# The last gates of the second group meet w_out as a split product in the third group's first period; weight splitting goes from two to three tiles a step

## The chip, the cores and the metric

One core of one Trainium2 chip runs the program. The metric is the device time of one execution in microseconds (us). Runs of one kernel differ by some us, so kernels are compared by the ratio of times taken in the same rounds.

In lines of the profile PE is TensorE (the matrix engine) and PEld its weight loads, DVE is VectorE, ACT is ScalarE, POOL is GpSimd, and SPq is the queue that issues the transfers. PSUM is the memory into which TensorE writes its sums. The granted clock is the share of its full clock that TensorE was given, 1.00 at most.

## The reference

```python
# q, k, v: (8, 8, 576, 64); w_in: (512, 2048), w_out: (2048, 512), both float64 in memory
kv  = einsum('bhsd,bhse->bhde', k, v)
out = einsum('bhsd,bhde->bhse', q, kv)
x   = out / sqrt(mean(out*out, -1) + 1e-6) * g_norm     # -> (4608, 512)
h   = x @ w_in
g   = h * erf(softplus(h))
y   = g @ w_out
```

## The kernel before

Tokens are taken in nine groups of 512. Hidden units come in 16 tiles of 128 (`FC`), four of them a batch (`BATCH`). Groups one and two use plain fp32 products. A full fp32 product of 128x128 by 128x512 is two records in the trace. From group three on each product is a Karatsuba split: every operand is held as a high part, a low part and their scaled sum, and three products of the rounded type fp32r replace one fp32 product. `n_ps` gathers two of them and `m_ps` the third.

A step is the work on one hidden tile; steps 0 to 15 are group one, 16 to 31 group two. In group two each step also splits two weight tiles. ACT rounds the high part (`w_upper`), VectorE makes the others one step later (`w_lower`), and a DMA writes the result to memory, from where the later groups load it. The stage through which this passes is a pool of buffers. Attention of the next group is woven into the steps, four steps for a pair of heads.

```python
    def w_upper(which, f):
        t = stage.tile([P, 3, G], FP32R, name="w_new", tag="w_new")
        ...
        upper(x, parts[:, 0])                       # ACT
        w_new[which, f] = t, x, [parts[:, i] for i in range(3)]

    def w_lower(which, f):
        t, x, parts = w_new.pop((which, f))
        lower(x, *parts)                            # VectorE, two instructions
        nc.vector.tensor_scalar(out=t[:, 1], in0=t[:, 1].bitcast(FP32),
                                scalar1=-SHIFT, scalar2=None, op0=ALU.mult)
        kept = w_kept[which, f] = dram.tile([P, 3, G], FP32, name=f"w_{which}{f}")
        nc.sync.dma_start(out=kept, in_=t.bitcast(FP32))
    ...
    for n in range(FIRST * FC + LAG):               # FIRST = 2 groups, LAG = 5 steps
        ...                                         # attention pieces of the next group
        if T < FIRST:
            ...                                     # h_ps: four fp32 products
            nc.scalar.copy(h, h_ps)
            nc.scalar.activation(s, h, AF.Softplus)
            for key in list(w_new):
                w_lower(*key)
            if T == FIRST - 1:
                for _ in range(2):
                    w_upper(*to_cut.pop(0))
            if f % BATCH == BATCH - 1:
                ...                                 # erf of the batch, tables
        if n >= LAG:
            T2, f2 = divmod(n - LAG, FC)
            project(f2, hs[n - LAG])                # o_ps: four fp32 products with w_out
            if f2 == FC - 1:
                store_first(T2)                     # out of PSUM and to memory, 1 MB
    ...
    for m in range(first_batch, batches + 1):       # a period: one batch of a later group
        for i in range(BATCH):
            n_ps, m_ps = hidden(T, b * BATCH + i)   # split products with w_in
            ...
        for j in range(J):                          # split products of the last period's gates
            if old_h is not None:
                result(T2, b2, j, g, w)
```

Each engine takes its instructions in the order written. The Trainium skill says it too ("TensorE: Matmul & The Clock Gate", section "Architectural detail: the array is 16× 32×32, not 1× 128×128": ACT and DVE queues are "strict FIFO").

## Time and profile before

| | before |
|---|---|
| time, median of 6 runs | 993.26 us (991.29 to 994.35) |
| TensorE busy, share of the profiled span of 990.5 us | 96% |
| VectorE, ACT busy | 75%, 62% |
| second group (130 to 262 us), TensorE busy | 131.91 of 132.00 us |
| second period of group three | 30.8 us, where a settled one takes 25.2 |

TensorE is the bound, the second group has no slack left on it, and the only thin place in the middle is the second period of group three. The first three of the six runs (median 994.19) are those the prediction knew.

### The profile page before, as it was taken

Reading aid. Unit: us, or ns where it says so; the run is one execution under the profiler, and the core shown is the slowest. Engines: PE = TensorE matmul, PEld = TensorE weight load, DVE = VectorE, ACT = ScalarE, POOL = GpSimd, SP = SyncE. Lnnn points to the kernel's source line nnn. Section 1 sums busy time; section 2 is a strip of 40 time slices with the busy share of each in tenths; the row PEclk is TensorE's granted clock in tenths of the full one; section 3 lists DMA queues with packets and bytes.
Section 4 is the critical chain, followed back from the end, with each engine's and each line's share of the span. In section 5 each row is a group of like instructions: output and inputs, shape, how many; then the busy total and the mean of one; then the engine's idle time right before and its main releaser. Section 6 shows DMA issues by size and latency. Waiting matters only on the chain.

```text
span 990.5 us, 11723 instructions
## 1 busy us (share of the span) xinstructions
PE 950.1 (96%) x4312; PEld 675.6 (68%) x4312; DVE 740.7 (75%) x1067; ACT 617.4 (62%) x821; POOL 2.4 (0%) x10
## 2 busy tenths in 40 slices
PE   6779999999998999999999999999999999989997
PEld 4334444444456778787778787878787787768885
DVE  2887896666845877777888777877778778886666
ACT  3688775677645666666666666666666666665551
POOL 0000000000000000000000000000000000000000
PEclk9899999999999999999999999999999999999999
DMA  9755514665679877898779877987796678657952
GB/s 273 233 165 165 164 41 176 251 235 226 272 268 381 312 280 266 262 368 294 274 244 355 310 283 241 347 304 284 248 330 254 252 257 337 264 222 295 358 200 74
DMA packets 100361, 256.63 MB, mean 259 GB/s; under 512 B 43984, under 2 KB 57296, under 8 KB 100304
## 3 DMA queue, kind: packets, MB, share of 16 engines
q1 hardware_dynamic: 98672, 253.59, 71.7%
q10 hardware_dynamic: 1568, 2.29, 0.8%
q8 instruction: 34, 0.56, 0.2%
q14 instruction: 23, 0.19, 0.1%
q0 software_dynamic: 64, 0.00, 0.0%
HBM read 221.25 MB, written 34.60 MB: 258 GB/s over the span
## 4 chain that ended last, share of the span: by engine, by line
PE 76%; DVE 14%; ACT 7%; DMA 2%; issue 1%; DVEq 0%
PE n_ps L411 32%; PE m_ps L411 16%; PE o_ps L451 10%; PE h_ps L573 9%; PE se_ps L302 3%; DVE e L394 3%; DVE h L693 2%; PE qt_ps L296 2%; PE kv_ps L274 2%; DVE h L394 1%; DVE u L342 1%; ACT s L675 1%; ACT s L680 1%; DVE x L351 1%; DVE u L339 1%
## 5 line engine op out<-in xcount | busy, mean ns | idle before, releaser
L411 PE MATMUL n_ps<-x_forms,w_in_parts 128*128 128x512 f32 x896 | 233.3, 402 | 3.0 <-ACT x_forms L376 2.8
L411 PE MATMUL n_ps<-w_out_parts,g_forms 128*128 128x512 f32 x896 | 223.3, 391 | 3.1 <-DMA w_out_parts<-w_out 3.1
L411 PEld LDWEIGHTS n_ps<-x_forms,w_in_parts 128*128 128x128 f32 x896 | 166.7, 188 | 47.5 <-issue 9.3
L411 PEld LDWEIGHTS n_ps<-w_out_parts,g_forms 128*128 128x128 f32 x896 | 169.0, 189 | 39.6 <-DMA w_out_parts<-w_out 3.9
L675 ACT ACTIVATE s<-h 128x512 f32<-128x512 f32 x112 | 70.8, 632 | 198.3 <-DVE h L394 198.3
L573 PE MATMUL h_ps<-xT,w_in_sb 128*128 128x512 f32 x256 | 119.8, 611 | 4.0 <-DVE qT L339 2.7
L411 PE MATMUL m_ps<-w_out_parts,g_forms 128*128 128x512 f32 x448 | 120.5, 391 | 0.0
L411 PE MATMUL m_ps<-x_forms,w_in_parts 128*128 128x512 f32 x448 | 120.0, 390 | 0.0
L394 DVE SCALAR_TENSOR_TENSOR h<-m_ps,h 128x512 f32<-128x512 f32 x112 | 77.1, 688 | 55.6 <-ACT h L673 45.5
L451 PE MATMUL o_ps<-w_out_sb,h_sb 128*128 128x512 f32 x256 | 114.8, 592 | 0.0
L379 DVE TENSOR_TENSOR g_forms<-h,g_forms 128x1024 fp32r<-128x1024 f32 x56 | 68.4, 1222 | 44.8 <-ACT g_forms L376 44.4
L411 PEld LDWEIGHTS m_ps<-w_out_parts,g_forms 128*128 128x128 f32 x448 | 84.4, 188 | 17.6
L411 PEld LDWEIGHTS m_ps<-x_forms,w_in_parts 128*128 128x128 f32 x448 | 84.1, 188 | 17.6
L573 PEld LDWEIGHTS h_ps<-xT,w_in_sb 128*128 128x128 f32 x256 | 49.2, 195 | 61.9 <-issue 54.1
L394 DVE SCALAR_TENSOR_TENSOR e<-m_ps,e 128x512 f32<-128x512 f32 x112 | 77.5, 692 | 16.9 <-PE m_ps L411 8.8
L451 PEld LDWEIGHTS o_ps<-w_out_sb,h_sb 128*128 128x128 f32 x256 | 48.6, 190 | 60.4 <-issue 56.4
L673 ACT ACTIVATE h<-n_ps 128x512 f32<-128x512 f32 x112 | 65.5, 585 | 18.9 <-PE n_ps L411 18.9
L394 DVE SCALAR_TENSOR_TENSOR e<-n_ps,e 128x512 f32<-128x512 f32 x84 | 57.5, 685 | 25.2 <-PE n_ps L411 25.2
L380 DVE SCALAR_TENSOR_TENSOR g_forms<-g_forms 128x1024 fp32r<-128x1024 f32 x56 | 68.6, 1225 | 1.9
L693 DVE TENSOR_TENSOR h<-h,s 128x1024 f32<-128x1024 f32 x56 | 65.9, 1218 | 3.1 <-ACT s L680 3.1
L376 ACT ACTIVATE g_forms<-h 128x1024 fp32r<-128x1024 f32 x56 | 58.9, 1052 | 7.8 <-DVE h L693 6.4
L103 ACT ACT_TABLE_LOAD x46 | 59.0, 1283 | 0.8
(80 smaller groups left out, 965.2 us busy)
## 6 DMA issues: line engine op xcount, KB each, us to landing
w_in_parts<-w_in SPq DMA_DIRECT2D x112, 768.0 KB, 6.3
w_out_parts<-w_out SPq DMA_DIRECT2D x112, 768.0 KB, 7.6
w_in<-w_new SPq DMA_DIRECT2D x16, 768.0 KB, 3.2
w_out<-w_new SPq DMA_DIRECT2D x16, 768.0 KB, 3.3
k_sb<-in_k_dram SPq DMA_DIRECT2D x29, 288.0 KB, 4.1
v_sb<-in_v_dram SPq DMA_DIRECT2D x29, 288.0 KB, 5.0
q_sb<-in_q_dram SPq DMA_DIRECT2D x32, 256.0 KB, 4.0
w_raw<-in_moe_w_out_dram SPq DMA_DIRECT2D x8, 1024.0 KB, 5.0
```

What stands on the lines that cost most here:

```text
L103: nc.scalar.preload_act_table_set("softplus")
L302: nc.tensor.matmul(o_ps, lhsT=bd, rhs=qT, start=True, stop=True)
L376: nc.scalar.activation(high, x, AF.Copy, scale=1.0 + 2.0**-13)
L379: nc.vector.tensor_tensor(out=low, in0=x, in1=high.bitcast(FP32), op=ALU.subtract)
L380: nc.vector.scalar_tensor_tensor(out=both, in0=low.bitcast(FP32), scalar=SHIFT, in1=high.bitcast(FP32), op0=ALU.mult, op1=ALU.add,)
L394: nc.vector.scalar_tensor_tensor(out=out_, in0=ps, scalar=scale, in1=out_, op0=ALU.mult, op1=ALU.add)
L411: nc.tensor.matmul(ps, lhsT=weights(form, k), rhs=moving(form, k), start=(form == forms[0] and k == 0), stop=(form == forms[-1] and k == 3),)
L451: nc.tensor.matmul(o_ps[j], lhsT=g[:, j * P : j * P + P], rhs=w_out_sb[:, f, :], start=(f == 0), stop=(f == FC - 1),)
L573: nc.tensor.matmul(h_ps, lhsT=w_in_sb[:, c, f * P : f * P + P], rhs=xT[T][:, c, :], start=(c == 0), stop=(c == KC - 1),)
L673: nc.scalar.activation(h[:, i], n_ps, AF.Copy, scale=1.0 - 1.0 / SHIFT)
L675: nc.scalar.activation(s[:, i], h[:, i], AF.Softplus)
L693: nc.vector.tensor_tensor(out=h[:, part], in0=h[:, part], in1=s[:, part], op=ALU.mult)
```

## The change

Four gate tiles (28 to 31) of group two stay back. They meet w_out as split products in the first period of group three, which had no such products of its own. The aim is cheaper products, and a first period that is like every other. For this the split weights must be in memory earlier, so three tiles are split a step, with five stage buffers instead of four. The split is scaled so that VectorE needs two instructions a tile instead of three, and the adds of `m_ps` out of PSUM need no factor. All tiles of w_in are now split before those of w_out. The rest of the change, cut here, moves buffers and the last attention pieces to make room.

```diff
-        upper(x, parts[:, 0])
+        upper_w(x, parts[:, 0])
...
-        lower(x, *parts)
-        nc.vector.tensor_scalar(
-            out=t[:, 1], in0=t[:, 1].bitcast(FP32), scalar1=-SHIFT, scalar2=None, op0=ALU.mult
-        )
+        lower_w(x, *parts)
...
-    to_cut = [(which, f) for f in range(FC) for which in ("in", "out")]
+    to_cut = [(which, f) for which in ("in", "out") for f in range(FC)]
+    whole = FIRST * FC - BATCH
-    for n in range(FIRST * FC + LAG):
+    for n in range(FIRST * FC + 1):
...
-            stage = stage_room.enter_context(tc.tile_pool(name="stage", bufs=4))
+            stage = stage_room.enter_context(tc.tile_pool(name="stage", bufs=5))
...
+            h = hs[n] = old_h[:, n - whole] if n >= whole else unit("h_sb")
...
             if T == FIRST - 1:
-                for _ in range(2):
-                    w_upper(*to_cut.pop(0))
+                for key in to_cut[:2]:
+                    w_upper(*key)
+                if not w_new and stage_room is not None:
+                    ...
+                    load_parts("in", BATCH)
...                                                 # erf of a batch, late attention pieces
+            if T == FIRST - 1:
+                for key in to_cut[2:3]:
+                    w_upper(*key)
+                del to_cut[:3]
...
+    load_parts("out", BATCH)
     for m in range(first_batch, batches + 1):
...
-            add_scaled(h[:, i], m_ps, 1.0 / SHIFT)
+            add(h[:, i], m_ps)
...
-            if old_h is not None:
-                result(T2, b2, j, g, w)
+            result(T2, b2, j, g, w)
```

More of the change, by code (lines that the diff above doesn't have):

```diff
@@ L86 @@
     dram = ctx.enter_context(tc.tile_pool(name="dram", bufs=1, space=bass.MemoryType.DRAM))
+    wide = ctx.enter_context(tc.tile_pool(name="wide", bufs=2, side="right"))
     room, early_room = (ctx.enter_context(ExitStack()) for _ in range(2))
     first_w = room.enter_context(tc.tile_pool(name="first_w", bufs=1, side="right"))
-    xp = room.enter_context(tc.tile_pool(name="xp", bufs=2, side="right"))
     gate = room.enter_context(tc.tile_pool(name="gate", bufs=7, side="right"))
@@ L346, in norm @@
                 if T not in xT:
-                    xT[T] = xp.tile([P, KC, G], FP32, name="xT", tag="xT")
+                    xT[T] = wide.tile([P, KC, G], FP32, name="xT", tag="h")
                 x = xT[T][:, p, :]
@@ L391, in thirds, with upper_w, lower_w @@
         lower(x, high, low, both)
+    def upper_w(x, high):
+        nc.scalar.activation(high, x, AF.Copy, scale=(1.0 + 2.0**-13) / SHIFT)
+    def lower_w(x, high, low, both):
+        nc.vector.scalar_tensor_tensor(
+            out=low, in0=high.bitcast(FP32), scalar=SHIFT, in1=x, op0=ALU.mult, op1=ALU.subtract
+        )
+        nc.vector.tensor_tensor(
+            out=both, in0=high.bitcast(FP32), in1=low.bitcast(FP32), op=ALU.subtract
+        )
     def add_scaled(out_, ps, scale):
@@ L396, in add_scaled, with add @@
         )
+    def add(out_, ps):
+        nc.vector.tensor_tensor(out=out_, in0=ps, in1=out_, op=ALU.add)
     banks = [(ps_h, "h"), (ps_h, "h")] + [(ps_o, f"o{i}") for i in range(4)]
@@ L445, with project @@
     o_ps = {}
-    def project(f, g):
+    def project(f, g, last):
         for j in range(J):
@@ L455, in project @@
                 start=(f == 0),
-                stop=(f == FC - 1),
+                stop=last,
             )
@@ L466, in store, with sums @@
             side.dma_start(out=out[first_row : first_row + R, :], in_=e[h * R : h * R + R, :])
-    def store_first(T):
+    es = {}
+    def sums():
         for j in range(J):
-            e = acc.tile([P, DM], FP32, name="e", tag="e")
+            e = es[j] = acc.tile([P, DM], FP32, name="e", tag="e")
             if j % 2:
@@ L474, in store_first @@
                 nc.vector.tensor_copy(out=e, in_=o_ps[j])
-            store(T, j, e)
     def unit(name):
@@ L504 @@
     }
+    w_seq["out"][:0] = [("out", f) for f in range(FC - BATCH, FC)]
     def load_parts(which, n):
@@ L517, in pieces_of @@
     def pieces_of(T):
-        steps = [[] for _ in range(FC + 1)]
+        steps = [([], []) for _ in range(FC + 1)]
         for p in range(NP):
-            products, apply, halve, mean, norm, split = attention(T, p)
-            for i, piece in enumerate((products, apply, halve, mean)):
-                steps[BATCH * p + (min(i + 1, 3) if T == 1 and p == 0 else i)].append(piece)
-            steps[BATCH * p + BATCH][:0] = [norm, split]
+            *four, norm, split = attention(T, p)
+            for i, piece in enumerate(four):
+                step = BATCH * p + i
+                if T == 1 and p == 0:
+                    step = min(i + 1, 3)
+                late_in = 0
+                if T == FIRST and p == NP - 1 and i == 3:
+                    step, late_in = step - 1, 1
+                steps[step][late_in].append(piece)
+            if T == FIRST and p == NP - 1:
+                steps[FC - 1][0].extend((norm, split))
+            else:
+                steps[BATCH * p + BATCH][0][:0] = [norm, split]
         return steps
-    to_cut = [(which, f) for f in range(FC) for which in ("in", "out")]
+    to_cut = [(which, f) for which in ("in", "out") for f in range(FC)]
     hs, ss = {}, {}
-    for n in range(FIRST * FC + LAG):
+    whole = FIRST * FC - BATCH
+    for n in range(FIRST * FC + 1):
         T, f = divmod(n, FC)
@@ L537 @@
             stage_room = ctx.enter_context(ExitStack())
-            stage = stage_room.enter_context(tc.tile_pool(name="stage", bufs=4))
-        if f == 0:
-            if T:
-                ends[0]()
-                if T < FIRST:
-                    ends[1]()
-            if T < FIRST:
-                if T + 1 == FIRST:
-                    x_forms[FIRST] = late.tile([P, 3, KC, G], FP32R, name="x_forms0")
-                *steps, ends = pieces_of(T + 1)
-        if T < FIRST:
-            for piece in steps[f]:
+            stage = stage_room.enter_context(tc.tile_pool(name="stage", bufs=5))
+            x_forms[FIRST] = late.tile([P, 3, KC, G], FP32R, name="x_forms0")
+        if T < FIRST:
+            if f == 0:
+                ends = steps[FC][0] if T else []
+                steps = pieces_of(T + 1)
+                steps[0][0][:0] = ends
+            for piece in steps[f][0]:
                 piece()
@@ L552 @@
             weights()
-        if n == FIRST * FC:
-            for key in list(w_new):
-                w_lower(*key)
-            stage_room.close()
-            w_in_p = ctx.enter_context(tc.tile_pool(name="w_in_p", bufs=BATCH))
-            load_parts("in", BATCH)
         done = n - LAG + 1
-        if 0 <= done < FIRST * FC:
+        if 0 <= done < whole:
             nc.vector.tensor_tensor(out=hs[done], in0=hs[done], in1=ss[done], op=ALU.mult)
-        if n == FIRST * FC + BATCH - 1:
-            ends[1]()
-        if n == FIRST * FC:
-            *steps, split = attention(FIRST + 1, 0)
-        elif T == FIRST:
-            for i in (f - 1,) if f < BATCH else (f - 1, f):
-                steps[i]()
         if T < FIRST:
@@ L579 @@
                 )
-            h, s = hs[n], ss[n] = unit("h_sb"), unit("s_sb")
+            if n == whole:
+                old_h = wide.tile([P, BATCH, G], FP32, name="h", tag="h")
+            h = hs[n] = old_h[:, n - whole] if n >= whole else unit("h_sb")
+            s = ss[n] = unit("s_sb")
             nc.scalar.copy(h, h_ps)
@@ L585 @@
             if T == FIRST - 1:
-                for _ in range(2):
-                    w_upper(*to_cut.pop(0))
+                for key in to_cut[:2]:
+                    w_upper(*key)
+                if not w_new and stage_room is not None:
+                    stage_room.close()
+                    stage_room = None
+                    w_in_p = ctx.enter_context(tc.tile_pool(name="w_in_p", bufs=BATCH))
+                    load_parts("in", BATCH)
             if f % BATCH == BATCH - 1:
@@ L591 @@
                 softplus_table()
+            for piece in steps[f][1]:
+                piece()
+            if T == FIRST - 1:
+                for key in to_cut[2:3]:
+                    w_upper(*key)
+                del to_cut[:3]
         if n >= LAG:
             T2, f2 = divmod(n - LAG, FC)
-            project(f2, hs[n - LAG])
-            if f2 == FC - 1:
-                store_first(T2)
+            last = n - LAG in (FC - 1, whole - 1)
+            project(f2, hs[n - LAG], last)
+            if last:
+                sums()
+                if T2 == 0:
+                    for j in range(J):
+                        store(T2, j, es.pop(j))
+    for n in range(whole, FIRST * FC):
+        nc.vector.tensor_tensor(out=hs[n], in0=hs[n], in1=ss[n], op=ALU.mult)
     room.close()
@@ L601 @@
     late_r = ctx.enter_context(tc.tile_pool(name="late_r", bufs=1, side="right"))
-    gate_r = ctx.enter_context(tc.tile_pool(name="gate_r", bufs=2, side="right"))
+    gate_r = ctx.enter_context(tc.tile_pool(name="gate_r", bufs=1, side="right"))
     w_out_p = ctx.enter_context(tc.tile_pool(name="w_out_p", bufs=7, side="right"))
@@ L614, in cut @@
         return t
-    es = {}
     def result(T, b, j, g, w):
@@ L626, in result @@
             nc.vector.tensor_scalar(
-                out=es[j], in0=ps[0], scalar1=1.0 - 1.0 / SHIFT, scalar2=None, op0=ALU.mult
+                out=es[j], in0=ps[0], scalar1=SHIFT - 1.0, scalar2=None, op0=ALU.mult
             )
         else:
-            add_scaled(es[j], ps[0], 1.0 - 1.0 / SHIFT)
-        add_scaled(es[j], ps[1], 1.0 / SHIFT)
+            add_scaled(es[j], ps[0], SHIFT - 1.0)
+        add(es[j], ps[1])
         if b == NB - 1:
             store(T, j, es.pop(j))
-    FETCH = (("in",) * 4 + ("", "out", "out", "out out"), (*("", "in", "in", "out"), *("in", "out", "in", "out out")))
-    old_h = None
+    FETCH = ("", "in", "in", "out", "in", "out", "in", "out out")
+    load_parts("out", BATCH)
     for m in range(first_batch, batches + 1):
@@ L641 @@
         if T + 1 < NG:
-            todo = list(attention(T + 1, b)) if m > first_batch else [split]
+            todo = list(attention(T + 1, b))
             if b == 0:
@@ L657, in fetch @@
         def fetch(place):
-            for which in FETCH[m > first_batch][place].split():
+            for which in FETCH[place].split():
                 load_parts(which, 1)
@@ L663 @@
         if m < batches:
-            h = gate_r.tile([P, BATCH, G], FP32, name="h", tag="h")
-            s = gate_r.tile([P, BATCH, G], FP32, name="s", tag="s", bufs=1)
+            h = wide.tile([P, BATCH, G], FP32, name="h", tag="h")
+            s = gate_r.tile([P, BATCH, G], FP32, name="s", tag="s")
         for i in range(BATCH):
@@ L669 @@
             fetch(i)
-            if old_h is not None and i < 2:
+            if i < 2:
                 g.append(cut(old_h, i))
             if m < batches:
-                nc.scalar.activation(h[:, i], n_ps, AF.Copy, scale=1.0 - 1.0 / SHIFT)
-                add_scaled(h[:, i], m_ps, 1.0 / SHIFT)
+                nc.scalar.activation(h[:, i], n_ps, AF.Copy, scale=SHIFT - 1.0)
+                add(h[:, i], m_ps)
                 nc.scalar.activation(s[:, i], h[:, i], AF.Softplus)
@@ L682 @@
                 softplus_table()
-        if old_h is not None:
-            T2, b2 = divmod(m - 1, NB)
-            w = [w_now["out", b2 * BATCH + f].pop(0).bitcast(FP32R) for f in range(BATCH)]
+        T2, b2 = divmod(m - 1, NB)
+        w = [w_now["out", b2 * BATCH + f].pop(0).bitcast(FP32R) for f in range(BATCH)]
         for j in range(J):
-            if old_h is not None:
-                result(T2, b2, j, g, w)
+            result(T2, b2, j, g, w)
             fetch(BATCH + j)
```

## The prediction

> **What bounds the kernel now.** I first read the busy shares of the page, then the busy times of each engine in stretches, then the chain of waits in order of time around the change, and last the instructions of TensorE there. The page gives the bound:
>
> ```profile
> PE 950.1 (96%) x4312; PEld 675.6 (68%) x4312; DVE 740.7 (75%) x1067; ACT 617.4 (62%) x821; POOL 2.4 (0%) x10
> ```
>
> TensorE (PE) is busy 96% of the 990.5 us, and its granted clock is 9 tenths or more nearly throughout, so only two things move the end: less matmul time, or fewer gaps on TensorE. The stretches (start:end, length, busy us of PE, PEld, DVE, ACT, POOL, granted clock, DMA share, GB/s) say where gaps are:
>
> ```profile
> 266.65:290.50 23.85, 23.85 (x85) 11.46 (x84) 11.60 (x22) 13.38 (x20) 0.00 (x0) 1.00 0.68 254
> 290.50:301.40 10.90, 10.90 (x50) 8.72 (x50) 4.08 (x7) 5.29 (x9) 0.00 (x0) 1.00 0.81 283
> 301.40:332.20 30.80, 27.26 (x161) 21.22 (x160) 22.36 (x30) 21.43 (x27) 0.00 (x0) 1.00 0.95 361
> 431.60:456.80 25.20, 25.19 (x133) 20.24 (x132) 20.07 (x30) 16.01 (x21) 0.00 (x0) 1.00 0.85 305
> ```
>
> The second group ends with a tail of plain fp32 products (266.65 to 290.50, TensorE full). Then the third group's first period does only its four hidden tiles (10.9 us), because no gates wait for it in split form. Its second period, the third row, takes 30.8 us where a settled one takes 25.2. In the chain of waits in order of time (start, us, what), the part that matters is:
>
> ```profile
> 263.38 3.43 PE h_ps L573 x8
> 266.81 6.87 PE o_ps L451 x16
> ...
> 275.22 3.44 PE o_ps L451 x8
> ...
> 279.74 6.87 PE o_ps L451 x16
> ...
> 287.07 3.43 PE o_ps L451 x8
> 290.50 1.85 PE n_ps L411 x8
> 292.35 0.91 PE m_ps L411 x4
> ...
> 302.90 1.28 ACT L680
> 304.19 2.02 ACT s L680 x2
> 306.22 1.28 ACT L103
> 307.52 0.64 ACT x_forms L376
> ```
>
> Here one fp32 step against w_out (four products, eight records) costs 3.43 us, and one split product with its n and m parts 1.85+0.91, or 1.81+0.91 = 2.72 us when settled. From 301 us on, the chain is no longer TensorE: the first period's erf and table load come straight before the second period's pieces, and TensorE waits for what is queued behind them. The timeline of TensorE gives the gaps in brackets:
>
> ```profile
> 310.02 0.43 PE L301 MATMUL kv_ps<-qT_last,bd_kv 128*128 128x64 f32 x2 [1.70 <-DVE bd_kv L289]
> 320.69 0.51 PE L323 MATMUL ms_ps<-sq_hi,mean_w 128*128 128x512 f32 x1 [1.11 <-DVE sq_hi L315]
> ```
>
> With 0.22, 0.18 and 0.34 us after these, 3.55 us is idle in that period.
>
> **What the Trainium skill says.** "VectorE: DVE Perf Modes", section "The perf-mode tier table (the rule you actually need)", gives tensor_scalar on fp32 in SBUF twice the base rate, tensor_tensor on fp32 only the base rate, and no gain on fp32 in PSUM. The trace agrees: the weight rescale (L437) takes 427 ns, tensor_tensor from SBUF (L379) 684, and tensor_scalar from PSUM (L626) 685. So turning the scaled add out of PSUM (688 ns) into a plain add saves nothing worth counting. "ScalarE: Activation LUTs", section "What ACT_TABLE_LOAD costs", gives 1283 ns and a drain of 1380 more for a switch. The trace has the 1283; the drain is not seen (a load from 269.16 ends at 270.44, erf starts at 270.45). "DMA: Bandwidth & Descriptors", section "Where 436 GB/s comes from", puts the fabric at 435 GB/s and HBM at some 358 per core. Here slices of 0.75 us between 200 and 230 us show up to 451 GB/s, so the measured figures decide, and I work with 400 as the ceiling that bursts can hold.
>
> **The change, part by part.**
>
> 1. Gates 28 to 31 of the second group no longer meet w_out in fp32 but split, in period one of the third group. Removed: 4 steps x 3.43 = 13.73 us of TensorE. Added: four results (one per 128 rows of output), each a split product: 4 x 2.72 = 10.88 us. TensorE saves 2.85 us, all of it on the path. Added elsewhere: two more cuts of the gates (ACT 2 x 1.05, DVE 2 x (1.22+1.22) = 4.9 us) and eight adds of about 0.69; they lie beside the hidden tiles as in every later period.
>
> 2. The first period becomes an ordinary one: hidden tiles, cuts, the next group's attention and four results. The order of instructions built from the changed kernel confirms that results now stand between hidden tiles of period one and those of period two, and that the last x parts are cut before the tail. This takes away the crowding that cost 3.55 us of gaps. From kv of period one to kv of period three I therefore count two settled periods, 2 x 25.2 = 50.4 us (two measured periods, 406.41 to 456.80, are 50.39 together). Before it stand steps 26 and 27 in fp32, 2 x 3.43 = 6.87; after it the kv and qt pieces up to the hidden tile, 1.6 (456.80 to 458.40). Sum 58.9 us. Before, the same work, from 266.65 to 332.20, took 65.55. Saving 6.7 us: 2.85 from the cheaper products, 3.55 from the gaps, some 0.3 from smaller ones.
>
> 3. Weight splits: three tiles a step for 11 steps instead of two for 16. VectorE loses the rescale, 32 x 0.427 = 13.7 us. Per step it has 3 x 1.38 = 4.15 us of splitting instead of 2 x 1.81 = 3.62, ACT 1.84 instead of 1.23. A step of TensorE is 30.45/4 = 7.6 us (160.98 to 191.43), and in 130 to 262 us TensorE is busy 131.91 of 132.00, so this stage has nothing to win. What it may lose: the tile of kv (bd_kv) was ready at 184.93, TensorE used it at 186.92; one more cut of 0.6 us ahead of it in ACT's queue leaves about 1.4 us. Writes: 3 x 0.786 MB in 7.6 us is 310 GB/s, with q, k, v some 340; below those 400. I count 0, with a tail to the bad side.
>
> 4. The copies of the four sums, the four late gate products, and new scales: copies 2 x 0.58 on ACT and 2 x 0.69 on DVE as before. Scaled parts change numbers and not counts, so 0.
>
> 5. Loads of the four w_out parts for period one. In the order of issues they wait for VectorE's last gate product, because their room is the old gates' room. Counting from the last fp32 hidden tile: fp32 steps end at 6.9; copies and four products of 0.69 on VectorE end at 9.6; first load out at 9.7. TensorE wants the parts at 6.9+1.5 (kv, qt)+4 x 2.72+1.1 (apply) = 20.4. That is 10.7 us for 3.1 MB; at 400 GB/s 7.9 us plus the 2 to 3 us that a load alone takes (3.2 for 0.786 MB). Just enough; I charge 0.3 us.
>
> Sum: 994.2 - 6.7 + 0.3 = 987.8, less a little for the spare VectorE time (0.2): **987.6 us**, 0.7% faster.
>
> **Rivals.** (a) A DMA wait takes the place of the crowding. For: DMA share 0.95 in the old second period, and median landing of a w_out load is 7.6 us on the page; period one carries 3.1 MB more than a settled one. Against: the first four w_in parts now load long before, while the engines of transfer idle (several empty slices in 285 to 320 us). It would leave 1 to 3 us at the first result, time 989 to 990.5. (b) Three splits a step throttle the second group: ACT waits for a stage buffer, the gate copies come late, TensorE stalls in each of three or four steps. For: at each fourth step ACT already has table, erf and softplus together. Against: 1.4 us of slack left and the writes below the ceiling. It would cost 1 to 4 us, time 988.5 to 991.5. (c) VectorE in period one is the bound: cut, hidden adds and late gate products queue up, and hi and lo of the mean come late. For: in the settled period hi and lo are ready (447.28) only 0.8 us before use (448.06). Against: the cut starts 3.7 us after kv by the count of part 5, the settled one 4.4 us after (436.06 from 431.62). It would return 1 to 1.5 us. (d) Gaps return fully and only 2.85 us stay: 991.3.
>
> **Range and chances.** Middle 987.6. The four rivals are one-sided, 1 to 4 us each and perhaps one in five each; better than counted is limited to about 2 us. The three runs before spread over 0.6 us. So 985.3 to 990.6 should hold 8 times in 10. Two per cent would be 19.9 us, more than everything that is touched; faster by over 2% 0.01, within 2% 0.98, slower 0.01.
>
> **What would show it.** Right: o_ps records 224 instead of 256, the n_ps and m_ps results 4 more tiles; no fp32 result after the second step behind the last h_ps; from that h_ps to the third period's first hidden tile 58 to 60 us; the 1.70 and 1.11 us gaps gone; still almost no idle TensorE from 130 to 262 us; the end of the kernel unchanged with its 3.1 us wait for w_out parts. Wrong: a bracket on the first n_ps of period one's results naming w_out_parts (a), brackets on kv_ps L303 or h_ps in the second group (b), one on ms_ps L325 in period one (c), or a settled period that is no longer 25.2 us, since I assume that nothing there changes.

## The result, and the profile after

| | before | after |
|---|---|---|
| time, median of 6 runs | 993.26 us | 991.13 us (989.59 to 993.23) |
| ratio | | 0.9981 (95%: 0.9965 to 0.9998) |

A ratio here is the mean time of one kernel's runs over the mean of the other's runs of the same rounds, so it is not quite the ratio of the medians. The gain is 0.2%, some 2 us; 0.7% had been predicted, and 991.13 lies above the range.

First, where in the program do the two traces part? The moment at which TensorE starts the mean of each pair of heads (ms_ps) is a good milestone, because it comes once a batch in both:

| milestone | before, us | after, us | after minus before |
|---|---|---|---|
| in the second group, pair two of the third group's attention | 201.33 | 201.49 | +0.16 |
| in the second group, pair three of the third group's attention | 231.89 | 236.93 | +5.04 |
| in group three, its third period | 347.05 | 345.30 | -1.75 |
| last pair of the eighth group | 775.62 | 773.45 | -2.17 |
| third pair of the ninth group | 847.27 | 845.13 | -2.14 |
| fourth pair of the ninth group | 871.55 | 870.43 | -1.12 |

Between the first and the second line something takes 4.9 us. Then the change gives back 6.8 us (from +5.04 to -1.75). Then little happens for 500 us. The busy times of the second group after the change (start:end, length, busy us of PE, PEld, DVE, ACT, POOL, granted clock, DMA share, GB/s), and those of the new first and second period:

```profile
130.00:262.00 132.00, 129.30 (x407) 59.78 (x406) 88.60 (x140) 85.95 (x127) 0.00 (x0) 0.99 0.64 250
278.55:303.62 25.07, 25.07 (x133) 20.17 (x132) 18.99 (x29) 16.07 (x22) 0.00 (x0) 1.00 0.87 325
303.62:328.82 25.20, 24.93 (x131) 20.09 (x130) 19.94 (x29) 16.02 (x21) 0.00 (x0) 1.00 1.02 365
```

The periods are settled ones, as intended: 25.07 and 25.20 us. The second group, full before, has lost 2.70 us of TensorE. TensorE's timeline after the change shows where (start, us, engine, line, what, count, in brackets the idle time before and who ended it):

```profile
220.71 0.43 PE L303 MATMUL kv_ps<-qT_last,bd_kv 128*128 128x64 f32 x2 [1.92 <-DVE qT_last L294]
220.99 1.46 PE L304 MATMUL se_ps<-qT,bd_kv 128*128 128x512 f32 x2
222.24 4.95 PE L582 MATMUL h_ps<-xT,w_in_sb 128*128 128x512 f32 x8
```

There is one gap of 1.92 us (0.37 and 0.34 us came shortly before it), and the eight h_ps records behind it take 4.95 us, where the same eight take 3.60 elsewhere. In the kernel before there is no gap at this place:

```profile
217.48 0.33 PE L301 MATMUL kv_ps<-qT_last,bd_kv 128*128 128x64 f32 x2
217.65 1.08 PE L302 MATMUL se_ps<-qT,bd_kv 128*128 128x512 f32 x2
218.56 3.60 PE L573 MATMUL h_ps<-xT,w_in_sb 128*128 128x512 f32 x8
```

Following the chain of waits in order of time back from that gap gives the cause:

```profile
198.76 0.70 DVE w_new L402
...
199.51 5.42 DMA w_in<-w_new
...
205.02 0.63 ACT w_new L396
205.65 0.02 issue
205.67 1.28 ACT L102
...
217.38 0.63 ACT w_new L396
218.01 0.53 ACT x_forms L378
...
219.99 0.13 DVE bd_kv L291
...
220.71 0.43 PE kv_ps L303 x2
```

A write of a split tile to memory, 5.42 us long here, holds ACT before the next tile. ACT then does the mean, the gates and the erf late, in their order. At 217.92 it rounds the x parts; before the change it did so at 212.93:

```profile
212.93 0.63 ACT L376 ACTIVATE x_forms<-x 128x512 fp32r<-128x512 f32 x1
```

VectorE copies bd_kv and qT_last behind that, and TensorE needs both. The waits of ACT between 180 and 225 us after the change (engine, line, for whom, us in total, times, longest):

```profile
ACT w_new L396 <- DMA w_in<-w_new: 6.3, 3, 3.8
ACT w_new L396 <- DVE e L490: 4.6, 1, 4.6
```

The four waits end at 191.16, 199.32, 203.12 and 205.02 us, in steps 20, 21 and 22. The wait of 4.6 us the profile puts down to a copy of VectorE that came last. By the times it is a write as well: VectorE finished the first tile of the step before at 187.7, its write was issued at 187.82, a write took 3.2 us before the change, and ACT went on at 191.16. And the memory traffic in two stretches, first of the kernel before, then after the change:

```profile
203.00:208.00 5.00, 5.00 (x13) 2.28 (x12) 3.33 (x6) 4.77 (x8) 0.00 (x0) 1.00 0.82 328
208.00:213.00 5.00, 5.00 (x38) 2.72 (x37) 0.00 (x0) 4.94 (x8) 0.00 (x0) 1.00 0.07 14
```

```profile
203.00:208.00 5.00, 5.00 (x13) 2.16 (x12) 3.68 (x6) 3.55 (x5) 0.00 (x0) 1.00 1.02 426
208.00:213.00 5.00, 4.29 (x36) 2.30 (x35) 2.14 (x3) 4.89 (x8) 0.00 (x0) 1.00 1.01 420
```

After the change the DMA engines run full, at 420 GB/s, up to 213 us. Before, they were done by 208. The median write of a split tile took 3.2 (w_in) and 3.3 us (w_out) from issue to landing before, 4.3 (w_in) and 5.2 (w_out) after.

**Theory A:** with three tiles a step the third tile needs the buffer of the previous step's first tile. That tile's write is not done in steps 20 to 22, the more so as the first group's results (1 MB) leave at the same time. ACT stands before it, and everything that ACT does later comes late. **Rival B:** the missing gain is lost to a clock that slows by chance, mostly in the last group. The profiled run shows such places (granted clock 0.91 from 880 to 900 us). **Rival C:** three splits are too much work for ACT and VectorE, whatever the buffers do.

### The profile page after: what moved, and what is told of

Read it like the earlier page. It is cut to its first block, busy times and chain, and to the rows that moved or that the text cites. A ratio compares the mean times of both kernels' runs of the same rounds, so it can differ in the third digit from the quotient of the medians.

```text
span 991.4 us, 11745 instructions
## 1 busy us (share of the span) xinstructions
PE 951.9 (96%) x4328; PEld 681.5 (69%) x4328; DVE 736.6 (74%) x1047; ACT 618.7 (62%) x822; POOL 2.4 (0%) x10
## 3 DMA queue, kind: packets, MB, share of 16 engines
q10 hardware_dynamic: 1568, 2.29, 0.8%
## 4 chain that ended last, share of the span: by engine, by line
PE 72%; DVE 15%; ACT 7%; DMA 3%; issue 2%; SPq 0%; DVEq 0%; ACTq 0%
PE n_ps L427 34%; PE m_ps L427 17%; PE h_ps L582 7%; PE o_ps L464 6%; DVE h L718 3%; PE se_ps L304 3%; DVE e L412 2%; PE qt_ps L298 2%; PE kv_ps L276 1%; DMA w_out_parts<-w_out 1%; DVE u L344 1%; DVE x L353 1%; DVE u L341 1%; DVE e L407 1%; ACT L105 1%
## 5 line engine op out<-in xcount | busy, mean ns | idle before, releaser
L427 PE MATMUL n_ps<-w_out_parts,g_forms 128*128 128x512 f32 x928 | 232.7, 393 | 3.0 <-DMA w_out_parts<-w_out 3.0
L427 PEld LDWEIGHTS n_ps<-w_out_parts,g_forms 128*128 128x128 f32 x928 | 175.6, 189 | 41.1 <-DMA w_out_parts<-w_out 3.8
L427 PE MATMUL m_ps<-w_out_parts,g_forms 128*128 128x512 f32 x464 | 125.0, 391 | 0.0
L412 DVE TENSOR_TENSOR h<-m_ps,h 128x512 f32<-128x512 f32 x112 | 77.1, 688 | 50.4 <-ACT h L700 47.1
L381 DVE TENSOR_TENSOR g_forms<-h,g_forms 128x1024 fp32r<-128x1024 f32 x58 | 70.9, 1223 | 46.9 <-ACT g_forms L378 46.6
L464 PE MATMUL o_ps<-w_out_sb,h_sb 128*128 128x512 f32 x224 | 100.5, 592 | 0.0
L427 PEld LDWEIGHTS m_ps<-w_out_parts,g_forms 128*128 128x128 f32 x464 | 87.8, 189 | 18.4
L412 DVE TENSOR_TENSOR e<-m_ps,e 128x512 f32<-128x512 f32 x116 | 80.3, 692 | 17.5 <-PE m_ps L427 9.3
L407 DVE SCALAR_TENSOR_TENSOR e<-n_ps,e 128x512 f32<-128x512 f32 x88 | 60.3, 686 | 28.8 <-PE n_ps L427 28.8
L464 PEld LDWEIGHTS o_ps<-w_out_sb,h_sb 128*128 128x128 f32 x224 | 42.5, 190 | 53.2 <-issue 49.5
L105 ACT ACT_TABLE_LOAD x45 | 57.7, 1283 | 0.8
```

What stands on the lines that cost most here:

```text
L105: nc.scalar.preload_act_table_set("softplus")
L381: nc.vector.tensor_tensor(out=low, in0=x, in1=high.bitcast(FP32), op=ALU.subtract)
L407: nc.vector.scalar_tensor_tensor(out=out_, in0=ps, scalar=scale, in1=out_, op0=ALU.mult, op1=ALU.add)
L412: nc.vector.tensor_tensor(out=out_, in0=ps, in1=out_, op=ALU.add)
L427: nc.tensor.matmul(ps, lhsT=weights(form, k), rhs=moving(form, k), start=(form == forms[0] and k == 0), stop=(form == forms[-1] and k == 3),)
L464: nc.tensor.matmul(o_ps[j], lhsT=g[:, j * P : j * P + P], rhs=w_out_sb[:, f, :], start=(f == 0), stop=last,)
```

## The experiments

All were run on one chip, each in five rounds with the kernel before. All gave correct results.

**1. The changed kernel once more.**

> The changed kernel once more, on the chip of the runs beside it. Theory A: ACT stands before a full stage (the third split tile of a step needs a buffer whose write to memory is not done), the tile bd_kv of the third pair of the third group's attention comes late, and TensorE loses about 5 us in the second group (2.6 us of gaps, the rest a slower clock after them). It expects the gap of about 1.9 us on kv_ps L303 again and a ratio to before of 0.998. Rival B: the missing gain is lost late, to clock dips in the last group that fall by chance. It expects other runs to show other times, with ratios from 0.993 to 0.999, and no steady gap in the second group.

Measured: 990.33 us median, ratio 0.9981 (0.9963 to 0.9999). The gap is there again. In this profile, however, no slow products follow:

```profile
222.81 0.43 PE L303 MATMUL kv_ps<-qT_last,bd_kv 128*128 128x64 f32 x2 [1.93 <-DVE qT_last L294]
223.09 1.08 PE L304 MATMUL se_ps<-qT,bd_kv 128*128 128x512 f32 x2
224.00 3.60 PE L582 MATMUL h_ps<-xT,w_in_sb 128*128 128x512 f32 x8
```

From pair two to pair three it is 33.76 us here, 35.44 in the first profile, and 30.56 before the change. So the stall costs 3.2 us in both profiles, and 1.7 us more in the one in which the clock falls behind it. In the first profile the granted clock was 0.50 from 222 to 224 us, and the slow stretch lasted about 3.4 us in all (221.5 to 225 us). The Trainium skill names such a gate ("TensorE: Matmul & The Clock Gate", section "What's actually happening") with a free-running window of some 3.4 us. In the ten kept traces, after the first 100 us, every slow stretch with products in it follows a gap of TensorE, and longer gaps have one more often: all 9 gaps of 2.6 us or more, 3 of the 16 from 1.6 to 2.0 us, 2 of the 35 from 1.0 to 1.3 us. This fits a window that does not start with the gap; that it is this window no run here shows. Rival B has a part in the spread between runs, not in the steady loss.

**2. Two tiles in steps 20 to 23.** The write traffic is thinned where the results leave; the splits end one step later.

```diff
+                each = 2 if FC + BATCH <= n < FC + 2 * BATCH else 3
                 for key in to_cut[:2]:
                     w_upper(*key)
...
-                for key in to_cut[2:3]:
+                for key in to_cut[2:each]:
                     w_upper(*key)
-                del to_cut[:3]
+                del to_cut[:each]
```

> The changed kernel, but only two tiles are split in steps 20 to 23, where the first group's results leave; the splits end one step later. Theory A expects no gap over 0.5 us on TensorE from 140 to 262 us, the third period's first hidden tile about 6.7 us earlier than before (325.5 instead of 332.2), and about 4.9 us less than the changed kernel: ratio to before about 0.993. Rival B expects the same time as the changed kernel within 1 us. Rival C (three splits a step are too much for ACT and VectorE themselves) expects most of the stall to move to step 28 and a gain under 2 us.

Measured: 985.83 us median, ratio 0.9934 (0.9921 to 0.9947). No wait of TensorE is left from 130 to 262 us, ACT waits 0.2 us for w_new in all, and pair two to pair three takes 30.56 us, exactly as before the change. The third period's first hidden tile starts at 324.83 us, where 325.5 was expected. The stretch over most of the second group:

```profile
130.00:255.00 125.00, 124.90 (x402) 58.38 (x401) 87.80 (x140) 85.63 (x127) 0.00 (x0) 1.00 0.61 239
```

This is what theory A asked for within 0.1%, and it speaks against rival B. The stall does not move to step 28 either, as rival C would have had it, though three tiles a step are split in eight of the twelve steps. The DMA engines still move 416 to 423 GB/s from 188 to 203 us here, so full transfers alone do no harm.

**3. Three tiles a step, the first group's results stored at step 28.**

```diff
-                if T2 == 0:
-                    for j in range(J):
-                        store(T2, j, es.pop(j))
+        if n == whole:
+            for j in range(J):
+                store(0, j, es.pop(j))
```

> The changed kernel with three splits a step, but the first group's four stores (1 MB) wait until step 28. If the write bandwidth is what fills the stage (theory A, bandwidth), the waits of ACT for w_new on a write fall from 13 us to under 5 and the gap on kv_ps L303 goes: 4 to 5 us less than the changed kernel, ratio about 0.993. If the number of stage buffers against the time of one write is what holds (theory A, buffers), the waits stay above 8 us and the gap shrinks but stays: 1 to 3 us less. Rival C (engine time) expects no change.

Measured: 987.13 us median, ratio 0.9950 (0.9936 to 0.9963). The gap on kv_ps fell from 1.92 to 0.71 us. The waits of ACT for w_new from 180 to 225 us:

```profile
ACT w_new L396 <- DMA w_out<-w_new: 4.8, 1, 4.8
ACT w_new L396 <- DVE e L490: 4.6, 1, 4.6
ACT w_new L396 <- DMA w_in<-w_new: 3.0, 2, 1.7
```

Of these the 4.8 us fall behind the critical chain (at 223 us). The changed kernel has the same wait in the same step, 24, up to 225.95 us, and no gap of TensorE follows it. So one such wait alone does no harm; in steps 20 to 22 the waits add up to 10.9 us, just before ACT has the mean, the tables and the erf to do. From pair two to pair three it takes 31.54 us here, 1.0 more than before the change; in the changed kernel it was 3.2 more. The 1 MB of results is worth about 3 us of the 5, the rest is the buffer that is asked for too soon: the wait of 4.6 us, in step 20, is unchanged, since it comes before the results leave. The answer is between the two forms of theory A. The waits on a write, 13.0 us from 130 to 275 us after the change, fall only to 11.0, as the form with the buffers had it; the gain is just over its 1 to 3 us. A sixth buffer would have been the direct test, but there is no room for it (36 KB a partition wanted, 32.2 left), so how much one more buffer alone would give stays open.

**4. The split alone, in the kernel before.** Scaled parts, three tiles a step, five buffers; the fp32 tail and the first period are as before.

> The kernel before with the new split alone (scaled parts, three tiles a step, five stage buffers, w_in first), its fp32 tail and its first period unchanged. Theory A expects the same stall in the second group and nothing gained elsewhere: 4 to 5 us more than before, ratio 1.004 to 1.005. Rivals B expects 1.000.

Measured: 997.42 us median, ratio 1.0050 (1.003 to 1.007). The gap is there with 1.93 us and the same 4.6, 3.8 and 4.7 us as ACT's longest waits; pair two to pair three takes 35.43 us, so the clock fell here too. The split alone explains the loss.

**5. The scaled parts alone, in the kernel before** (two tiles a step).

> The kernel before with the scaled parts alone: two VectorE instructions a weight tile instead of three (13.7 us of VectorE less), plain adds out of PSUM, two tiles a step as before. VectorE is not on the path in the second group, so both theories expect the time of before within 0.1%: ratio 0.999 to 1.001, no gap on TensorE from 140 to 262 us.

Measured: 993.20 us median, ratio 1.0006 (0.9991 to 1.0022). It is the same time, and no wait of TensorE in the second group. The scaled form is neither a gain nor the cause.

**6. The third tile rounded by GpSimd.** Writes and buffers are unchanged; only the engine that has to wait is another.

```diff
-        upper_w(x, parts[:, 0])
+        if third:
+            nc.gpsimd.tensor_scalar(
+                out=parts[:, 0], in0=x, scalar1=(1.0 + 2.0**-13) / SHIFT, scalar2=None, op0=ALU.mult
+            )
+        else:
+            upper_w(x, parts[:, 0])
```

> The changed kernel with three splits a step; the rounding of the third tile alone moves from ACT to GpSimd, which is idle. Writes and buffers stay as they are. If ACT standing in order before a full stage is what makes bd_kv late (theory A), ACT no longer waits on the third tile, the gap on kv_ps L303 (1.9 us) goes or falls under 0.5 us, and the time is 3 to 5 us under the changed kernel: ratio 0.993 to 0.995, if GpSimd rounds a 128x512 tile in under some 4 us. If VectorE's own load or the writes make bd_kv late whatever ACT does (rival C), the gap stays above 1.5 us and the ratio is 0.998.

Measured: 986.25 us median, ratio 0.9938 (0.9925 to 0.9952). No wait of TensorE is left in the second group. GpSimd took 1.49 us for a w_in tile at the median, and stood before DMA writes for 21.5 us in all. ACT still waited 6.2 us for its own two tiles, in six pieces of 1.4 us at most, without harm. So it is the order on ACT that carried the wait to TensorE: with the same three splits on VectorE and the same bytes the loss is gone. This rules out rival C for VectorE and for the writes by themselves. ACT has 0.6 us a step less to do here, and in steps 20 to 23 of experiment 2 as well, so these two runs alone do not exclude ACT's own work. Other figures speak against it. Four times 0.6 us is 2.4, while the x parts came 5.0 us late and ACT had stood still for 10.9 us before. In experiment 3 ACT has all its work and the gap shrinks to 0.71 us. In steps 24 to 27 of experiment 2 ACT rounds three tiles a step and no gap follows.

**7. The kernel before with its fp32 tail, and the split of experiment 2.**

> The kernel before, with its fp32 tail and its first period, and the split as in the version with two tiles in steps 20 to 23. If the whole gain of that version (ratio 0.993) comes from the gates that meet w_out in the third group's first period, and the split only has to be kept from stalling, this kernel has the time of before: ratio 0.999 to 1.001, no gap on TensorE in the second group, the gaps of 1.7 and 1.1 us in the second period still there. If an early end of the split is worth something by itself, it is faster than before by 1 us or more.

Measured: 992.63 us median, ratio 1.0009 (0.9994 to 1.0025). The second group has no wait of TensorE, and the two main gaps in the second period stay:

```profile
PE kv_ps L301 <- DVE bd_kv L289: 1.7, 1, 1.7
PE ms_ps L323 <- DVE sq_hi L315: 1.1, 1, 1.1
```

So the whole gain of experiment 2 comes from the gates that meet w_out later, and none from the split.

**8. Experiment 2, with the last four w_out loads in the buffers of w_in.** This goes beyond the change and asks what a gap costs.

```diff
-        pool = w_in_p if which == "in" else w_out_p
...
+                spare = which == "out" and len(w_seq["out"]) < BATCH
+                pool = w_in_p if which == "in" or spare else w_out_p
```

> The version with two tiles in steps 20 to 23, and the last four w_out loads put into the buffers of w_in, which nobody needs any more at that point, so that the last period does not wait for a w_out buffer. In the version without it that wait is 2.75 us near the end and the following products run at a slower clock (n_ps 2.29 for five and m_ps 1.83 for four, instead of 1.3 and 1.07). If the clock falls because of the gap, taking the gap away returns 4 to 4.5 us: ratio about 0.989. If the slow clock comes there whatever the gap, it returns 2.7: ratio about 0.9905.

Measured: 982.19 us median (981.54 to 987.57), ratio 0.9906 (0.9888 to 0.9924); it beats both kernels. The wait for w_out parts went, and another that it had hidden took part of its place:

```profile
PE n_ps L427 <- DVE g_forms L381: 1.0, 1, 1.0
```

So 1.75 of the 2.75 us of gap went. Between the medians it returned 3.6 us. The slow n_ps and m_ps behind the gap (2.29 and 1.83 us) became 1.19 for four and 1.21, and the granted clock is 1.00 there, so in this profile the slow clock went with the gap. The ratio is the smaller of the two expected; but a gap of 1 us is left, and one of the six runs (987.57) had a clock of 0.988, the others 0.994. Of the 4.45 us that the gap and the slow clock cost together, 3.4 should come back with 1 us of gap left, which the 3.6 between the medians agrees with; 1.75 would come back if the slow clock came whatever the gap. The expectation "4 to 4.5 us" was a little too high.

## Why the prediction was wrong

**What bounds the kernel, and the saving of part 2: right.** From the last h_ps of the second group to the third period's first hidden tile it took 58.75 us (271.68 to 330.43); 58.9 was predicted, 65.55 it was before. Experiment 2, in which nothing disturbs this, gains 0.66%, or 6.6 us of 992.24; the predicted saving was 6.7. The o_ps records are 224, and the n_ps records with w_out 928 instead of 896, as the list of signs had them. Experiment 7 shows that this gain belongs to the moved gates.

**Part 1, 2.85 us by cheaper products: agrees with the trace.** The first results take 1.83+0.91 us each, as counted. How the 6.8 us divide between products and gaps was not tried by itself; it follows from the durations.

**Part 3, the weight splits: this step failed.** It said "I count 0". Its mistake was to compare a mean rate, 340 GB/s, with a ceiling of 400. Two things were left out. The first group's results leave in the same four steps: 12 tiles of 0.786 MB, 1.05 MB of results and about 1 MB of q, k and v are 11.5 MB in 30.45 us, or 377 GB/s on average, and from 193 to 213 us the DMA engines ran at 420 without a pause. And a mean says nothing of a buffer's round trip: five buffers for three tiles a step leave the third tile with the buffer that VectorE finished in the same step. The slack of 1.4 us that I found for bd_kv counted ACT's work, not ACT's waiting. Measured on TensorE: 3.2 us, and 4.9 where the clock falls too, instead of 0. By the times, 6.6 us of gain were forecast and some 2 came; experiment 4 puts the split alone at 0.5%, or 5 us. (The three runs from which the prediction started lay 0.9 us above the median of all six.)

**Rival (b) named the mechanism.** It had "ACT waits for a stage buffer", with 1 to 4 us and one chance in five. Its time, 988.5 to 991.5 us, held the measured 991.13, and the list of signs had its mark, a bracket on kv_ps L303 in the second group. What it got wrong is the place: one gap, not a stall in each of three or four steps, and TensorE waited there for bd_kv and qT_last, not for the gate copies. Where the clock fell as well, the cost was 4.9 us, above its 1 to 4, because a gap's cost does not end with the gap.

**Part 4 and the steady state: right.** Experiment 5 puts the scaled parts at 1.0006, and the settled period is still 25.2 us.

**Part 5 and rivals (a), (c), (d): as judged.** TensorE does not wait for w_out parts in the first period, nor for hi and lo there, and the gaps of the second period are gone. Of the 0.3 us charged nothing was seen. (The 3.2 us that the prediction takes for a load alone is the page's time of a write, w_in<-w_new; the loads on that page have medians of 6.3 and 7.6 us.)

**What the list of signs did not have** is the slow clock after a gap. In the first profile after the change it also took about 1 us between 845 and 870 us, where the kernel before had the same gap (1.26 us) without it, and the rest of the way from -1.12 to the +0.9 us with which that profile ended lies for the most part behind another gap (1.66 us, clock 0.83 from 880 to 890 us; 1.00 in the kernel before). The second profile of the same kernel has these gaps (1.26 and 1.67 us) at a clock of 1.00; the slow stretches are spread, not a cause.

## What to carry to other kernels

When work is packed more tightly into fewer steps, do not compare the mean rate of its writes with the bandwidth. Ask when the buffer that the next instruction needs comes round, what else leaves in just those steps, and which engine stands in order before it. If that engine also carries a chain to the bound engine, give the wait to an idle engine or thin the steps in which the other traffic leaves: either recovered the full gain here. And a gap on TensorE can cost almost double its width (1.92 us of gap and 1.7 us of slow clock), since the clock may fall behind it.

## What the Trainium skill lacked or had wrong

- "TensorE: Matmul & The Clock Gate", section "What's actually happening", gives one idle window of about 3.4 us as what slows the clock, and nothing for shorter gaps. Here gaps of 1.92, 1.29 and 2.75 us were followed by products at half clock (granted 0.50 from 222 to 224 us and from 847 to 849 us), and a gap of 1.93 us in another run was not. Over the ten traces it was 9 of 9 gaps of 2.6 us or more, 3 of 16 from 1.6 to 2.0 us and 2 of 35 from 1.0 to 1.3 us. What decides among the shorter ones no run here shows.
- "ScalarE: Activation LUTs", section "What ACT_TABLE_LOAD costs": the 1283 ns are right, the drain of 1380 ns after a switch does not show on either side of the load; it began 0.02 us after the instruction before it, and erf 0.01 us after it.
- "DMA: Bandwidth & Descriptors", section "Where 436 GB/s comes from", says that the HBM side, some 358 GB/s, binds between HBM and SBUF, though the largest transfer measured on the same page, by a single core, reached 425. Here, with one core at work, a mix of mostly writes held 420 GB/s from 193 to 213 us, so the 358 did not bind.
